# Another plan for a planned attention and MLP kernel: projections in row pieces, the first query masked by ScalarE, an exponential of zeros behind each Gelu

## The chip, the cores and the metric

The kernel runs on one core of a Trainium2 chip. A core has a matrix engine (TensorE, PE), a vector engine (VectorE, DVE), a scalar engine for activation functions (ScalarE, ACT), GpSimd (POOL), and a queue engine (SyncE, SP) that starts most transfers. The metric is the device time in microseconds from start to end of the program.

## The reference

Input x has 2048 rows of 512. One branch is an attention block with 32 heads of 16, the other a mixer MLP, and a gate mixes the two:

```
q, k, v = split(x @ wqkv)                  # 32 heads, 16 wide
a = softmax(q k^T / 4) v  @ wo             # 2048 x 2048 scores in each head
h = gelu(layernorm(x) @ w1);  hs = shift(h) @ w2;  x1 = x + hs
b = x1 + gelu(layernorm(x1) @ w3) @ w4     # 1792 wide inside
g = sigmoid(sum(x * gate_w));  out = g a + (1 - g) b
```

The scores are the bulk: 32 heads x 2048 x 2048 exponentials. The kernel cuts them into 2048 tiles of 128 keys x 512 queries.

## The kernel before

**Tiles.** A round is a chunk of 512 queries, a group of eight heads and one half of it (p); there are 32 rounds of 64 tiles. A score tile (`qk_op`, L1363; matmul on L1366) contracts over 32 rows, of which a mask leaves the 16 of one head: `qbuf` holds each query twice, once multiplied by `mE` and once by `mO`. Four score tiles can run at once on the four row tiles of TensorE (row mode). PV products and projections run as four 32-column pieces (column mode, L1590 and L999), four matmuls side by side making one step.

**Exponentials.** A tile goes one of two ways. ScalarE (`issue_act`, L1461) takes two neighbouring PSUM banks, 1024 columns, in one exponential, sometimes three or one. VectorE (`issue_dve`, L1492) writes the approximate bits of an exponential as a 16-bit integer, and three more copies shifted by multiples of 32 are made of each pair (`close_pair`), by VectorE (L1535) or GpSimd (L1537); the four PV products of these copies together approximate the exponential. So a VectorE tile costs four PV products and a ScalarE tile one.

**The rest.** Projections of q, k, v, the MLP (w1, w2, w3, w4) and the output are "gens": lists of column-mode steps into one PSUM bank, evacuated mostly by VectorE. A step over 128 rows can also be given as four 32-row pieces in row mode (`by_rows`, L1007), to row tiles that a group of scores leaves free (`Gen.row_piece`, L166); before, only the longest w4 gens can be. The first Gelu (L1233) covers all 2048 rows, the second (L1270) comes in two pairs of chunks, so ScalarE leaves its exponentials three times, and each time loads the Gelu table and then the exponential's again.

**What sets the order.** Nothing is scheduled by hand at the level of instructions. At build time a small event-driven model (`Sim`) plays the engines with fixed durations, and `pe_pick` decides at each free moment of TensorE what comes next: scores for ScalarE, scores for VectorE, PV products or a gen's steps, and fillers on zeros (L1923) where nothing is ready. The instructions are emitted in the model's order, and the hardware then runs each engine's queue in that order with semaphores. The decisions hang on knobs (`K`): a base set, and a table `STEPS` which changes some of them after every eight score tiles. For example GP3 decides how often a pair's last shifted copies stay on VectorE, DVE_STOP how many tiles of a round VectorE leaves alone at its end, ROWM how many steps a gen must have in hand before it gives one as row pieces (99 means never), SL0 and SL1 how far PE may run beyond the end of an exponential. The table was found by a search; it has 215 entries with 721 settings.

**The start.** `x_transposes` makes x^T of the first chunk, `q_proj` the first queries (16 matmuls), `k_first` the first keys in two halves of 256. The mask of the first query is split: VectorE takes columns 0 to 255 (L1086), ScalarE 256 to 511 (L1089), then ScalarE copies both key halves (L1056), and the first scores follow.

Of the kernel before, what the change touches and what calls it, by code (L numbers as in the profile page):

```python
# [452 lines left out]
def kernel(  # L453
# [87 lines left out]
        12: dict(AT_SH=0),
        13: dict(AGE=12000, ROWM=3),
        14: dict(P1_PRIO=0.312, S_PRIO=0.214, SL0=60, IDLE_NS=374, B_LOW=1, PRESS=11, MAXU=7, DUE_SH=0, HOLE=2, E_PRIO=2,
            AFIRST=2, AGE=20000, ROWM=99, ACC2=1, JOIN=0),
        16: dict(GP3=0.633, URG=2, ACC2=0),
        17: dict(GP3=0.967, DVE_STOP=6, URG=5, B_LOW=2, ACC2=1),
        18: dict(AHEAD2=16, MAXG=2),
        19: dict(SL1=130),
        20: dict(SL1=0),
        21: dict(P1_PRIO=0.279, GP2=1, GP3=0.9, DUE_SH=32),  # L550
        23: dict(GP2=0.5, ACC2=0),
        25: dict(GP3=0.633, AT_SH=69),
        26: dict(GP2=1, GP3=0.9, AT_SH=0, ACC2=1),
        27: dict(SL0=0, DUE_SH=-9),
        28: dict(DVE_STOP=13, JOIN=1),
        29: dict(DVE_STOP=6, JOIN=0),
        30: dict(ACC2=0),
        31: dict(ROT=0),
        32: dict(DVE_STOP=13, ROT=2, ACC2=1, JOIN=1),
        33: dict(P1_PRIO=0.136, AHEAD2=9),  # L560
        34: dict(P1_PRIO=0.279, AHEAD2=16),
        35: dict(ROT=3),
        36: dict(LIMA=4),
        37: dict(PV_IDLE=0.5, PRESS=18),
        41: dict(S_PRIO=0.38),
        44: dict(S_PRIO=0.178, SL1=-75, AHEAD2=24, AGE=12000),
        45: dict(ROT=1),
        46: dict(B_LOW=8),
        47: dict(GP3=0.8, DVE_STOP=4, EARLY=64, SL1=130, MAXU=2, AT_SH=118),
        48: dict(GP3=0.9, DVE_STOP=13, EARLY=99, SL1=-75, B_LOW=2, MAXU=7, ROT=3, AT_SH=0),  # L570
        50: dict(DVE_ALONE=500),
        51: dict(IDLE_NS=864, ROT=2),
        52: dict(GP3=0.967, DVE_STOP=4, DVE_STOP_L=12, URG=8, URG_L=18, DVE_ALONE=-158, IDLE_NS=700, B_LOW=3, DVE_WAIT=4,
            PV_FULL=0.916, PV_IDLE=0.117, PRESS=26, MAXU=3, ROT=0, DUE_SH=-14, AT_SH=118, HOLE=7, MAXG=1, E_PRIO=0.4,
            AFIRST=0, AGE=20000, ACC2=0, LIMA=3, JOIN=0),
        53: dict(HOLE=0),
        54: dict(DVE_ALONE=-81, MAXU=5, ROT=1),
        55: dict(URG=2, DVE_ALONE=138),
        56: dict(P1_PRIO=0.312),
        57: dict(S_PRIO=0.625, ROT=2),  # L580
        58: dict(E_PRIO=2),
        59: dict(GP2=0.655),
        60: dict(GP3=1, E_PRIO=0.4),
        61: dict(DVE_STOP_L=7, LIMD=4),
        62: dict(DVE_ALONE=2),
        63: dict(SL1=0),
        64: dict(DVE_STOP=13),
        65: dict(DVE_STOP=6, ROT=3, JOIN=1),
        66: dict(DVE_STOP=4, ROT=2, JOIN=0),
        67: dict(DVE_WAIT=3, HOLE=7),  # L590
        68: dict(GP2=1),
        69: dict(AHEAD2=13),
        70: dict(DVE_STOP_L=16, AHEAD2=24, ROT=1),
        71: dict(SL1=-75, ROT=3),
        72: dict(GP2=0.655, DVE_STOP_L=7, SL1=0, ROT=2),
        73: dict(GP2=1, AHEAD2=13),
        74: dict(P1_PRIO=0.136, S_PRIO=0.178, GP3=0.967, DVE_STOP=8, DVE_STOP_L=12, URG=5, DVE_ALONE=-158, SL1=-75,
            IDLE_NS=537, B_LOW=8, DVE_WAIT=4, AHEAD2=24, PV_IDLE=0.731, MAXU=3, ROT=3, DUE_SH=32, LIMD=3, E_PRIO=0.1,
            ROWM=7, LIMA=4),
        75: dict(S_PRIO=0.625),  # L600
        76: dict(S_PRIO=0.178),
        77: dict(LIMD=4, LIMA=2),
        79: dict(P1_PRIO=0.414, AFIRST=2, ROWM=5),
        80: dict(SL0=-75),
        82: dict(AGE=12000),
        84: dict(ROT=1),
        85: dict(HOLE=3),
        86: dict(URG=3, AFIRST=0),
        87: dict(B_LOW=0),
        88: dict(B_LOW=8),  # L610
        89: dict(B_LOW=0),
        90: dict(URG=5, B_LOW=8, AFIRST=2),
        91: dict(GP2=0.5),
        92: dict(GP2=0.8, ROT=0),
        93: dict(GP2=1, ROT=1),
        94: dict(DVE_STOP=4, DVE_WAIT=2),
        95: dict(DVE_STOP=8, DVE_STOP_L=7, DVE_WAIT=4, ROT=0),
        96: dict(GP3=0.9, DVE_ALONE=362, PRESS=18),
        97: dict(GP2=0.315, ROT=3),
        98: dict(GP2=1, ROT=0),  # L620
        99: dict(P1_PRIO=0.743, DVE_STOP_L=16, AT_SH=96, AFIRST=1),
        100: dict(P1_PRIO=0.414, GP3=0.8, DVE_STOP_L=7, ROT=1, AT_SH=118, AFIRST=2),
        101: dict(URG=11, ROWM=99),
        102: dict(P1_PRIO=0.312, GP2=0, GP3=0.967, DVE_STOP_L=12, URG=8, DVE_ALONE=500, SL1=-150, IDLE_NS=700, B_LOW=3,
            AHEAD=3, PV_FULL=0.813, PV_IDLE=0.5, PRESS=8, ROT=0, DUE_SH=-9, HOLE=0, CAP2=5, LIMD=3, E_PRIO=0.4, AGE=6000,
            ROWM=5, LIMA=3),
        105: dict(DVE_STOP=6),
        106: dict(P1_PRIO=0.414, AHEAD=5, LIMD=2),
        107: dict(LIMD=4),
        108: dict(P1_PRIO=0.312, GP3=1, URG=5, IDLE_NS=864, AHEAD=3, PV_IDLE=0.731, ROT=2, LIMD=3, AFIRST=1, LIMA=4,  # L630
            JOIN=1),
        109: dict(SL0=0, ACC2=1),
        110: dict(URG=8),
        112: dict(SL1=0, MAXG=2),
        113: dict(DVE_STOP=4),
        114: dict(S_PRIO=0.214, B_LOW=5, JOIN=0),
        116: dict(S_PRIO=0.178, IDLE_NS=537, B_LOW=3, JOIN=1),
        117: dict(PV_IDLE=0.5),
        118: dict(DVE_WAIT=2, ROT=3, DUE_SH=0),
        119: dict(P1_PRIO=0.279, GP2=0.315, GP3=0.967, URG=3, URG_L=12, DVE_ALONE=362, EARLY=64, SL0=-75, IDLE_NS=864,  # L640
            B_LOW=8, BRES=4, DVE_WAIT=3, AHEAD=9, PV_FULL=0.86, PV_IDLE=0.117, PRESS=18, MAXU=4, ROT=1, DUE_SH=-6,
            HOLE=3, MAXG=1, E_PRIO=2, AFIRST=0, AGE=20000, ROWM=7, ACC2=0, LIMA=3, JOIN=0),
        120: dict(GP3=0.8, DVE_ALONE=2),
        121: dict(SL1=-75, ROT=2),
        122: dict(GP2=0.15, GP3=0.967, URG=2, DVE_ALONE=138, SL1=0, BRES=0, DVE_WAIT=2, PV_FULL=0.947, ROT=1),
        123: dict(DVE_STOP=6, ROT=2, CAP3=6),
        124: dict(DVE_STOP=4, ROT=1, CAP3=0),
        125: dict(SL0=0, MAXU=3),
        126: dict(PRESS=11),
        127: dict(SL1=-75),  # L650
        129: dict(DVE_STOP=8, IDLE_NS=374, E_PRIO=0.25),
        130: dict(DVE_STOP=4, IDLE_NS=864, E_PRIO=2),
        131: dict(GP2=0.655, GP3=1, SL1=0, B_LOW=2, PV_FULL=0.97, PRESS=18, MAXU=4, E_PRIO=0.4),
        132: dict(DVE_STOP=8, CAP3=6),
        134: dict(ROT=3),
        136: dict(ROT=0),
        137: dict(CAP3=0),
        138: dict(SL0=-75),
        140: dict(P1_PRIO=0.312, ROT=3, DUE_SH=32),
        142: dict(P1_PRIO=0.279, ROT=0, DUE_SH=-6),  # L660
        144: dict(GP3=0.9, MAXU=3),
        145: dict(CAP2=6),
        146: dict(URG=11),
        147: dict(S_PRIO=0.38),
        148: dict(GP3=0.8),
        149: dict(GP3=0.9),
        150: dict(GP3=0.8),
        151: dict(GP2=0.8),
        152: dict(DVE_STOP=4),
        153: dict(GP3=0.9, PV_IDLE=0.5),  # L670
        155: dict(GP2=0),
        156: dict(GP2=0.8),
        157: dict(GP2=0),
        158: dict(GP2=0.8, GP3=0.8),
        160: dict(GP2=0.5),
        161: dict(GP2=0.8),
        164: dict(P1_PRIO=0.414, DVE_STOP=8, AHEAD2=16),
        165: dict(AHEAD2=13),
        166: dict(GP3=0.9),
        167: dict(P1_PRIO=0.136),  # L680
        168: dict(DVE_ALONE=-81),
        169: dict(DUE_SH=0),
        170: dict(SL0=0, IDLE_NS=459, AT_SH=69),
# [308 lines left out]
    def gen(name, at, deps, mms, N=512, due=None):  # L992
# [22 lines left out]
        if name == "w4" and len(mms) > 5:  # L1015
            g.by_rows = by_rows
# [1003 lines left out]
```

## Time and profile before

| | |
|---|---|
| median of 3 runs | 747.18 us (747.05 to 747.32) |
| the profiled execution | 746.63 us, its span 744.8 us |
| mean granted TensorE clock | 0.999 |
| TensorE, ScalarE, VectorE, GpSimd busy | 98%, 98%, 92%, 63% of the span |
| first exponential | 9.03 us |

Busy time on a page is time in which at least one instruction of the engine was under way, so where instructions overlap, the mean length of one times their number is more than the busy time. A group's row gives line, engine, operation, tiles and count, then the busy time in us and the mean length of one in ns, then the idle time before them and what ended it. A row of the timeline gives start and length in us of one instruction or of a merged run of equal ones, and in brackets the idle time before it.

### The profile page before, as it was taken

The page shows a single profiled execution, that of the slowest core. Times are in us where ns is not written, and L with a number is a line of the kernel's source. Part 1 is how long each engine was busy: PE and PEld are TensorE (multiplying, and loading weights), DVE is VectorE, ACT ScalarE, POOL GpSimd, SP SyncE. Part 2 cuts the span into 40 slices and gives each one's busy share as a digit, 9 for nine tenths or more (in the row PEclk, how much of TensorE's full clock was granted, in tenths as well). Part 3 has the DMA queues.
Part 4 walks back from the last instruction along what each step waited for, and adds up shares of the span by engine and source line. Part 5 has one row for each costly group of instructions (what it writes and reads, how often), then busy time and mean ns, then how long its engine had stood idle before and what let it go on. Part 6 is the DMA issues. An engine that isn't in the chain of part 4 may idle for free.

```text
span 744.8 us, 23763 instructions
## 1 busy us (share of the span) xinstructions
PE 732.9 (98%) x9539; PEld 215.9 (29%) x9539; DVE 682.8 (92%) x1417; ACT 730.2 (98%) x768; POOL 466.5 (63%) x464
## 2 busy tenths in 40 slices
PE   8999999999999999999999999999999999999997
PEld 5333322223322222223222222222222342222222
DVE  5999999999999999999998888999989879999996
ACT  7999999999999999999999999999999999999995
POOL 2456667778556676654566755477677785556562
PEclk9999999999999999999999999999999999999999
DMA  8512231231321220034000110011100000110001
GB/s 185 161 39 45 66 75 41 59 67 46 84 63 52 62 70 22 20 87 102 10 24 9 38 43 21 14 35 41 28 21 18 21 12 25 29 27 21 20 9 45
DMA packets 67094, 34.60 MB, mean 46 GB/s; under 512 B 46748, under 2 KB 62380, under 8 KB 66984
## 3 DMA queue, kind: packets, MB, share of 16 engines
q1 hardware_dynamic: 66040, 32.56, 17.5%
q8 instruction: 74, 1.21, 0.7%
q10 hardware_dynamic: 944, 0.52, 0.2%
q14 instruction: 36, 0.29, 0.1%
HBM read 17.40 MB, written 6.81 MB: 33 GB/s over the span
## 4 chain that ended last, share of the span: by engine, by line
PE 78%; ACT 12%; DVE 3%; issue 3%; POOL 2%; DMA 1%; SPq 0%; DVEq 0%; POOLq 0%; ACTq 0%
PE banks L1590 28%; PE banks L1366 27%; PE banks L999 22%; ACT prob L1461 11%; POOL prob L1537 1%; DVE prob L1535 1%; DVE prob L1492 1%; PE banks L978 0%; POOL oT L1629 0%; DMA pk<-den 0%; DMA bcs<-rr 0%; PE banks L1923 0%; SPq L1633 0%; PE banks L1030 0%; ACT L1461 0%
## 5 line engine op out<-in xcount | busy, mean ns | idle before, releaser
L1461 ACT ACTIVATE prob<-banks 128x1024 bf16<-128x1024 f32 x747 | 686.1, 1144 | 0.9 <-PE banks L1590 0.3
L1537 POOL TENSOR_SCALAR prob<-prob 128x1024 uint16<-128x1024 uint16 x402 | 413.5, 1046 | 240.5 <-DVE prob L1535 102.6
L1492 DVE TENSOR_SCALAR prob<-banks 128x512 uint16<-128x512 f32 x552 | 365.6, 684 | 31.1 <-PE banks L1366 24.9
L1590 PE MATMUL banks<-prob,V 128*17 128x512 bf16 (+1 forms) x3710 | 315.8, 381 | 0.6 <-POOL prob L1537 0.5
L1366 PE MATMUL banks<-q,kT 32*128 32x512 bf16 x2048 | 279.1, 384 | 4.8 <-ACT prob L1461 2.0
L1535 DVE TENSOR_SCALAR prob<-prob 128x1024 uint16<-128x1024 uint16 x429 | 166.9, 434 | 7.9 <-PE banks L1590 3.5
L1366 PEld LDWEIGHTS <-kT 32*128 32x128 bf16 x2048 | 70.6, 90 | 306.4 <-ACT prob L1461 279.1
L1590 PEld LDWEIGHTS <-V 128*17 128x17 bf16 (+1 forms) x3710 | 70.8, 88 | 118.2 <-issue 97.8
L999 PE MATMUL banks<-xnT,w 128*32 128x512 bf16 x1152 | 88.8, 383 | 0.1
L999 PE MATMUL banks<-w,hT 128*32 128x512 bf16 x688 | 59.5, 383 | 0.0
L999 PEld LDWEIGHTS <-w 128*32 128x32 bf16 x1936 | 41.0, 95 | 48.9 <-issue 28.6
L1629 POOL TENSOR_TENSOR oT<-accsb,bcs 128x512 bf16<-128x512 f32 x31 | 40.0, 1291 | 19.5 <-DVE prob L1535 9.1
L999 PE MATMUL banks<-w,w 128*32 128x256 bf16 (+1 forms) x784 | 38.8, 308 | 0.2
L999 PE MATMUL banks<-w,hB 128*32 128x512 bf16 x448 | 37.4, 382 | 0.3 <-DVE prob L1492 0.3
L1010 PE MATMUL banks<-wo,oD 32*128 32x512 bf16 x64 | 23.8, 384 | 0.0
L1611 DVE COPY accsb<-banks 128x512 f32<-128x512 f32 x31 | 21.2, 683 | 0.8 <-POOL oT L1629 0.2
L1174 DVE BATCH_NORM_STATS2 st<-x_sb 128x6 f32<-128x512 bf16 x32 | 21.3, 681 | 0.0
L999 PEld LDWEIGHTS <-hT 128*32 128x32 bf16 x688 | 14.8, 95 | 19.8 <-issue 13.1
L1263 DVE CAST hT<-banks 128x512 bf16<-128x512 f32 x28 | 19.0, 680 | 1.5 <-PE banks L999 1.5
L1263 DVE CAST hB<-banks 128x512 bf16<-128x512 f32 x28 | 19.1, 684 | 1.4 <-PE banks L999 1.3
L999 PE MATMUL banks<-w,wq 128*32 128x512 bf16 x256 | 19.6, 383 | 0.0
L999 PE MATMUL banks<-wo,oD 128*32 128x512 bf16 x176 | 19.5, 383 | 0.0
(95 smaller groups left out, 261.1 us busy)
## 6 DMA issues: line engine op xcount, KB each, us to landing
bcs<-rr SPq DMA_DIRECT2D x124, 64.0 KB
xn_dram<-xn SPq DMA_DIRECT2D x32, 128.0 KB
w<-in_B_w_dram SPq DMA_DIRECT2D x5, 512.0 KB
oD<-oT SPq DMA_DIRECT2D x124, 16.0 KB
w<-in_B_w_dram SPq DMA_DIRECT2D x4, 448.0 KB
out_dram<-ot SPq DMA_DIRECT2D x14, 128.0 KB
x_sb<-in_A_x_dram SPq DMA_DIRECT2D x3, 512.0 KB
w<-in_A_wqkv_dram SPq DMA_DIRECT2D x2, 256.0 KB
```

Of the source, the lines that this page charges most:

```text
L999: units.append([Op("col", j, lambda j=j, lf=lf, rf=rf, n0=n0, n1=n1, st=st, sp=sp: nc.tensor.matmul(get()[32 * j:32 * j + 32, n0:n1], lhsT ...
L1010: o = Op("row", i, lambda: nc.tensor.matmul(get(), lhsT=lf(0, P)[rows], rhs=rf()[rows], start=False, stop=True, tile_position=(32 * i, 0), ...
L1174: a = dve(600, deps, lambda: nc.vector.bn_stats(out=sb.slot[:], in_=x_sb[:, t, :]), prio=6, at=at, acq=[sb])
L1263: pre.append(evac(g, PSUM_NS, lambda ps, m=m: nc.vector.tensor_copy(out=h2()[:, m, :], in_=ps[:])))
L1366: o = Op("row", i, lambda: nc.tensor.matmul(dst(), lhsT=kT[G][32 * i:32 * i + 32, kt * P:(kt + 1) * P], rhs=qbuf[G, c].slot[32 * i:32 * i ...
L1461: job = act(hold, ops, lambda: nc.scalar.activation(out=prob[:, pb.cut(), :].bitcast(BF16), in_=unit()[:, rb.cut(), :], func=ACT.Exp, scal ...
L1492: return nc.vector.tensor_scalar(out=prob[:, b0.cut() if w == 2 else b0.bufs[h0].slot, :], in0=unit()[:, rb.cut() if w == 2 else rb.bufs[0 ...
L1535: return nc.vector.tensor_scalar(out=cut(k), in0=cut(0), scalar1=float(SHIFT * k), scalar2=None, op0=ALU.add)
L1537: return nc.gpsimd.tensor_scalar(out=cut(k), in0=cut(0 if both else 2), scalar1=1.0, scalar2=float(SHIFT * (k if both else 1)), op0=ALU.mu ...
L1590: return nc.tensor.matmul(one(accs[r])[32 * i:32 * i + n, :], lhsT=lhs(n), rhs=rhs(), start=st and not edge, stop=True, tile_position=(0, ...
L1611: e = dve(PSUM_NS, round_ops[r], lambda: nc.vector.tensor_copy(out=ab.slot[:], in_=one(accs[r])), acq=[ab], prio=0, frees=[accs[r], Call(a ...
L1629: n = gp(1250, d3, lambda: nc.gpsimd.tensor_tensor(out=ob.slot[:], in0=ab.slot[:], in1=bb.slot[:], op=ALU.mult), acq=[ob], frees=[ab, bb], ...
```

## The change

- The table STEPS is another one, from a short search: 184 entries with 413 settings. With it the order of nearly all the work and the split of tiles between the engines differ.
- `by_rows` is set for all gens whose name begins with w, k or q, that have more than three steps and are not of the start, instead of the long w4 gens alone.
- The mask of the first query is one ScalarE instruction over 512 columns; the first half of the first keys is copied by VectorE instead of ScalarE.
- Behind the first Gelu and behind the last Gelu of each pair, ScalarE runs an exponential of a column of zeros into a tile that is not needed any more. The model's durations for the Gelus are changed with it.

```diff
@@ STEPS (cut)
-        0: dict(GP2=0.8, DVE_STOP=13, DVE_ALONE=-158, SL0=130, B_LOW=2, PRESS=43, AGE=20000),
-        1: dict(PV_FULL=0.97, E_PRIO=0.4, JOIN=1),
...
+        81: dict(DVE_STOP=13, ROT=3, ROWM=1, ACC2=1),
+        82: dict(DVE_STOP=6, SL1=0, ROT=2, AT_SH=0, ROWM=99, ACC2=0),
...
+        124: dict(ROWM=1),
...
+        204: dict(ROT=3, AT_SH=96, ROWM=0),
...
@@ gen
-        if name == "w4" and len(mms) > 5:
+        if name[0] in "wkq" and len(mms) > 3 and at >= 0:
             g.by_rows = by_rows
@@ k_first
-            j = act(275, g.units[-1], lambda g=g, h=h: nc.scalar.copy(out=kT[0][:, 256 * h:256 * h + 256],
-                                                                      in_=one(g.buf)[:, 0:256]), prio=0, frees=[g.buf])
+            j = (act if h else dve)(275 if h else 345, g.units[-1], lambda g=g, h=h: (
+                nc.scalar.copy if h else nc.vector.tensor_copy)(out=kT[0][:, 256 * h:256 * h + 256],
+                                                                in_=one(g.buf)[:, 0:256]), prio=0, frees=[g.buf])
@@ q_proj
-            e1 = [dve(345, g.units[-1] + [j_m3], lambda: nc.vector.tensor_scalar(
-                out=qb.slot[:, 0, 0:256], in0=one(g.buf)[:, 0:256], scalar1=mE[:], scalar2=None, op0=ALU.mult), prio=0,
-                acq=[qb])]
-            e1.append(act(330, g.units[-1] + [j_m3], lambda: nc.scalar.activation(
-                out=qb.slot[:, 0, 256:512], in_=one(g.buf)[:, 256:512], func=ACT.Copy, scale=mE[:]), prio=0))
-            e1[1].need = qb
+            e1 = [act(535, g.units[-1] + [j_m3], lambda: nc.scalar.activation(
+                out=qb.slot[:, 0, :], in_=one(g.buf), func=ACT.Copy, scale=mE[:]), prio=-1, acq=[qb])]
@@ new, before mlp1
+    def gelu(ap, back):
+        g = nc.scalar.activation(out=ap, in_=ap, func=ACT.Gelu_apprx_tanh)
+        if back:
+            nc.scalar.activation(out=mb[:].bitcast(F32), in_=zero[:, 0:1], func=ACT.Exp)
+        return g
@@ mlp1
-        ge = act(93 + 1700 * KT + 3450, pre, lambda: nc.scalar.activation(
-            out=hT[:, :, 2:2 + S], in_=hT[:, :, 2:2 + S], func=ACT.Gelu_apprx_tanh), prio=0)
+        ge = act(93 + 1700 * KT + 2850, pre, lambda: gelu(hT[:, :, 2:2 + S], True), prio=0)
@@ mlp2
-            ge = act(93 + 427 * FT + (0 if n else 2750), pre, lambda h2=h2: nc.scalar.activation(
-                out=h2(), in_=h2(), func=ACT.Gelu_apprx_tanh), prio=-1)
+            back = n == len(cs) - 1
+            ge = act(93 + 427 * FT + (1310 if n == 0 else 0) + (1490 if back else 0), pre,
+                     lambda h2=h2, back=back: gelu(h2(), back), prio=-1)
```

More of the change, by code (lines that the diff above doesn't have):

```diff
@@ L541 @@
[L541 to L550, printed above, removed]
@@ L590 @@
[L590 to L599, printed above, removed]
@@ L600 @@
[L600 to L615, printed above, removed]
@@ new lines @@
+        1: dict(HOLE=3),
+        2: dict(AT_SH=118),
+        3: dict(AGE=12000),
+        4: dict(GP2=1, DVE_WAIT=1),
+        5: dict(GP2=0.5),
+        6: dict(AHEAD2=24),
+        7: dict(GP2=1, AHEAD2=13),
+        8: dict(AFIRST=1),
+        9: dict(ROT=3, DUE_SH=32, ACC2=1),
+        12: dict(DVE_STOP=8, URG=11),
+        13: dict(DVE_STOP=6, URG=5),
+        14: dict(LIMA=2),
+        18: dict(GP3=0.9),
+        20: dict(DVE_WAIT=4),
+        21: dict(SL1=-75, HOLE=2),
+        22: dict(SL1=60, HOLE=3),
@@ new lines @@
+        23: dict(SL1=-75, HOLE=2),
+        24: dict(GP2=0.5),
+        25: dict(ROT=1),
+        26: dict(MAXU=3),
+        27: dict(HOLE=3),
+        29: dict(HOLE=2),
+        30: dict(AHEAD=5),
+        32: dict(ROT=0),
+        33: dict(AHEAD=24, MAXG=2),
+        34: dict(AHEAD=5, MAXG=1, AFIRST=2),
+        35: dict(ROT=1),
+        37: dict(ACC2=0),
+        40: dict(URG=8),
+        43: dict(E_PRIO=0.1),
+        44: dict(E_PRIO=2),
+        45: dict(ROT=2),
+        46: dict(DVE_ALONE=-81, MAXU=7),
@@ new lines @@
+        60: dict(P1_PRIO=0.312),
+        61: dict(GP2=1),
+        63: dict(DVE_WAIT=1),
+        64: dict(PRESS=15, ROT=0),
+        65: dict(DVE_WAIT=4, PRESS=18, ROT=2),
+        66: dict(P1_PRIO=0.55),
+        67: dict(P1_PRIO=0.312),
+        69: dict(HOLE=7),
+        70: dict(DVE_STOP_L=12, IDLE_NS=459, B_LOW=8, JOIN=1),
+        72: dict(DVE_STOP_L=14, IDLE_NS=374, B_LOW=3, JOIN=0),
+        73: dict(ROT=1),
+        74: dict(DVE_STOP_L=12, IDLE_NS=459, B_LOW=8, ROT=2, JOIN=1),
+        76: dict(PV_FULL=0.813, MAXG=2),
@@ new lines @@
+        97: dict(GP3=0.9),
+        99: dict(E_PRIO=0.1),
+        101: dict(GP3=0.967),
+        102: dict(GP3=0.9, E_PRIO=2),
+        103: dict(AFIRST=0),
+        104: dict(GP2=0),
+        105: dict(DVE_ALONE=500),
+        106: dict(DUE_SH=-6),
+        108: dict(HOLE=7),
+        109: dict(MAXU=2),
+        111: dict(ROT=1),
+        112: dict(URG=3, SL0=-75, PV_IDLE=0.5),
+        113: dict(MAXU=9, LIMD=4, LIMA=4),
+        115: dict(GP3=1, MAXG=2),
+        116: dict(EARLY=64, PRESS=26, LIMA=2),
@@ new lines @@
+        126: dict(DVE_STOP_L=7, CAP2=5),
+        127: dict(DVE_STOP_L=14, CAP2=6),
+        128: dict(SL1=0),
+        129: dict(URG_L=18, SL0=0),
+        131: dict(DVE_WAIT=4, E_PRIO=0.25),
+        132: dict(AT_SH=118),
+        133: dict(ROT=1, AGE=3000),
+        134: dict(PV_FULL=0.86),
+        137: dict(PV_FULL=0.916, ROT=2, AGE=9000),
+        138: dict(PV_FULL=0.86, ROT=1, AGE=3000),
+        141: dict(PV_FULL=0.916, ROT=2, AGE=9000),
+        144: dict(GP2=0.8),
+        146: dict(BRES=2, AT_SH=0),
@@ new lines @@
+        148: dict(PV_FULL=0.813, GATE=3),
+        149: dict(GP2=0.655, GP3=1, BRES=0, PV_FULL=0.916, AT_SH=118, GATE=2),
+        150: dict(GP2=0.8, GP3=0.967),
+        151: dict(GP2=0, URG_L=12, SL0=45, SL1=60, DVE_WAIT=3, AT_SH=0, E_PRIO=2, ROWM=99),
+        152: dict(DVE_STOP=4, URG_L=18, PV_IDLE=0.117, MAXU=4),
+        153: dict(ROWM=3),
+        154: dict(URG=2),
+        155: dict(GP2=1, URG=5),
+        156: dict(AT_SH=118),
+        157: dict(AT_SH=0),
+        158: dict(LIMD=4),
+        160: dict(LIMD=3),
@@ new lines @@
+        161: dict(IDLE_NS=459, AHEAD=3),
+        162: dict(URG=3),
+        163: dict(URG=5),
+        164: dict(DVE_STOP=6, SL0=60),
+        165: dict(AFIRST=2),
+        166: dict(E_PRIO=0.4),
+        167: dict(GP2=0.655),
+        169: dict(GP2=0, URG_L=12, SL0=45, IDLE_NS=537, AHEAD=9, PV_IDLE=0.731, MAXU=9, E_PRIO=2, AFIRST=0, ROWM=99),
+        170: dict(GP2=1, URG_L=18, SL0=60, IDLE_NS=459, AHEAD=3, PV_IDLE=0.117, MAXU=4, AFIRST=2, ROWM=3),
+        171: dict(E_PRIO=0.4),
+        172: dict(S_PRIO=0.3, IDLE_NS=864),
@@ new lines @@
+        173: dict(P1_PRIO=0.279, AHEAD2=24),
+        176: dict(DVE_STOP_L=12, URG_L=12, ROT=0, AT_SH=96),
+        178: dict(URG=11, AT_SH=69, AFIRST=0),
+        179: dict(MAXG=2),
+        180: dict(URG=5, AT_SH=96, MAXG=1, AFIRST=2),
+        182: dict(AT_SH=34),
+        183: dict(S_PRIO=0.178),
+        184: dict(IDLE_NS=374, AT_SH=96),
+        185: dict(AHEAD=7),
+        186: dict(HOLE=0),
+        187: dict(URG=11, LIMD=4),
+        189: dict(DVE_ALONE=500),
+        190: dict(P1_PRIO=0.55, URG_L=18, SL0=0),
@@ new lines @@
+        192: dict(P1_PRIO=0.279, GP2=0.315),
+        193: dict(PRESS=8),
+        194: dict(AT_SH=118, AFIRST=0),
+        195: dict(SL0=-150, DUE_SH=32),
+        197: dict(P1_PRIO=0.414, S_PRIO=0.38, DVE_STOP_L=14, URG=5, URG_L=12, DVE_ALONE=2, SL0=45, IDLE_NS=537, AHEAD=9,
+            AHEAD2=13, PV_IDLE=0.731, PRESS=18, MAXU=9, ROT=2, DUE_SH=-14, AT_SH=0, HOLE=3, LIMD=3, E_PRIO=2, ROWM=99),
+        199: dict(GP2=0, HOLE=7),
+        200: dict(E_PRIO=0.4),
+        201: dict(GP2=1, E_PRIO=2),
@@ new lines @@
+        202: dict(AT_SH=34),
+        203: dict(AHEAD2=16),
+        204: dict(ROT=3, AT_SH=96, ROWM=0),
+        205: dict(DVE_STOP_L=7, ROT=0),
+        208: dict(GP2=0.315),
+        209: dict(GP3=0.8, AHEAD=12),
+        210: dict(GP2=0, GP3=0.967, DVE_STOP_L=14, AHEAD=9, AHEAD2=13, ROT=2, AT_SH=0, ROWM=99),
+        211: dict(ROWM=3),
+        213: dict(ROT=0, LIMA=4),
+        214: dict(PV_FULL=0.86),
+        217: dict(AHEAD=12, MAXU=2),
+        219: dict(S_PRIO=0.3, CAP2=5),
+        221: dict(ROT=3),
@@ new lines @@
+        225: dict(PRESS=8),
+        226: dict(S_PRIO=0.38, BRES=4, ROT=1),
+        227: dict(SL0=130),
+        228: dict(S_PRIO=0.3, SL0=45, BRES=0, MAXU=4, ROT=3),
+        229: dict(MAXU=2),
+        231: dict(S_PRIO=0.38, SL0=130, BRES=4, ROT=1),
+        232: dict(S_PRIO=0.3, GP2=0.315, SL0=45, SL1=-75, BRES=0, ROT=3),
+        233: dict(GP2=0, SL1=60, MAXU=4),
+        234: dict(MAXU=2),
+        235: dict(ROT=0),
+        237: dict(ROT=2),
+        240: dict(URG=11, URG_L=18),
+        241: dict(URG=5, URG_L=12),
```

238 lines of the change are left out of this document (39 added, 199 removed).

## The prediction

> **What bounds the kernel now.** I read the page's busy shares first, then the groups of instructions, then single stretches of the timeline, because three engines look full at once.
>
> ```profile
> span 744.8 us, 23763 instructions
> PE 732.9 (98%) x9539; PEld 215.9 (29%) x9539; DVE 682.8 (92%) x1417; ACT 730.2 (98%) x768; POOL 466.5 (63%) x464
> PE 78%; ACT 12%; DVE 3%; issue 3%; POOL 2%; DMA 1%; SPq 0%; DVEq 0%; POOLq 0%; ACTq 0%
> L1461 ACT ACTIVATE prob<-banks 128x1024 bf16<-128x1024 f32 x747 | 686.1, 1144 | 0.9 <-PE banks L1590 0.3
> ```
>
> The chain of waits gives 78% to TensorE, but matmuls are pipelined and follow each other through ScalarE's releases, so the chain alone cannot say which of the two is full. ScalarE's line can. The groups by form, the timeline and the list of waits:
>
> ```profile
> L1461 ACT ACTIVATE prob<-banks 128x1024 bf16<-128x1024 f32 x745 | 684.4, 1144 | 0.9 <-PE banks L1590 0.3 <-PE banks L1366 0.2
> L1461 ACT ACTIVATE prob<-banks 128x1536 bf16<-128x1536 f32 x1 | 1.5, 1458 | 0.0
> L1461 ACT ACTIVATE prob<-banks 128x512 bf16<-128x512 f32 x1 | 0.8, 778 | 0.0
> ...
> 360.65 1.02 ACT L1461 ACTIVATE prob<-banks 128x1024 bf16<-128x1024 f32 x1
> 362.47 13.87 ACT L1461 ACTIVATE prob<-banks 128x1024 bf16<-128x1024 f32 x15
> 460.05 13.89 ACT L1461 ACTIVATE prob<-banks 128x1024 bf16<-128x1024 f32 x15
> ...
> PEld L1366 <- ACT prob L1461: 279.1, 636, 1.4
> ```
>
> One exponential alone lasts 1.02 us; fifteen in a row last 13.87 us, so each further one adds (13.87 - 1.02) / 14 = 0.918 us. Over the whole run, 684.4 us of occupied time over 745 exponentials is 0.9187 us each. The mean of the run is the pace of an undisturbed stretch: apart from the 0.9 us of idle time shown, ScalarE is never late. Of the score groups on TensorE (702 in the built instruction stream of the kernel before), 636 wait for an exponential to free PSUM banks. So TensorE is paced by ScalarE, not the other way round, and the time is the number of exponentials times 0.9187 us, plus the Gelus with their table loads, the start and the end.
>
> **The change, part by part.** Counts of the changed kernel are from its built instruction stream; durations are from the profile.
>
> Other plan, exponentials. A tile of scores is exponentiated on ScalarE, or approximated on VectorE. ScalarE had 1494 of 2048 tiles (745 wide instructions, one of three tiles, one of one); now it has 1504, in 752 wide ones. VectorE has 544 instead of 554. ScalarE: 752 x 0.9187 = 690.9 us against the 686.1 us that all 747 took: +4.8 us. All of it is on the path, since that row has no idle time to fill. Bounds: +4.6 at 0.918 with nothing else, +4.8 at the mean; I take +4.8.
>
> Other plan, the other engines:
>
> ```profile
> L1492 DVE TENSOR_SCALAR prob<-banks 128x512 uint16<-128x512 f32 x550 | 363.3, 682 | 31.0 <-PE banks L1366 24.9 <-ACT prob L1461 1.7
> L1492 DVE TENSOR_SCALAR prob<-banks 128x1024 uint16<-128x1024 f32 x2 | 2.4, 1219 | 0.0
> L1535 DVE TENSOR_SCALAR prob<-prob 128x1024 uint16<-128x1024 uint16 x429 | 166.9, 434 | 7.9 <-PE banks L1590 3.5 <-ACT prob L1461 1.6 <-POOL prob L1537 0.6
> L1537 POOL TENSOR_SCALAR prob<-prob 128x1024 uint16<-128x1024 uint16 x402 | 413.5, 1046 | 240.5 <-DVE prob L1535 102.6 <-PE banks L1590 38.4 <-DVE prob L1492 24.6
> ...
> 164.84 0.61 PE L1590 MATMUL banks<-prob,V 128*17 128x512 bf16 x8
> 165.44 0.39 PE L1366 MATMUL banks<-q,kT 32*128 32x512 bf16 x2
> 165.75 0.61 PE L1590 MATMUL banks<-prob,V 128*17 128x512 bf16 x8
> 166.35 0.39 PE L1366 MATMUL banks<-q,kT 32*128 32x512 bf16 x3
> ```
>
> VectorE: single tiles 550 to 536 (14 x 363.3/550 = -9.2 us), double tiles 2 to 4 (+2.4), shifted copies 429 to 453 (24 x 166.9/429 = +9.3): +2.5 us on an engine with 62 us idle, so nothing directly. GpSimd: shifted copies 402 to 363, 39 x 413.5/402 = -40 us; it is 37% idle, so no gain. TensorE: groups in row mode 702 to 716, steps in them 708 to 730, column-mode steps 1825 to 1818. A group takes 0.31 us until column work starts behind it (165.44 to 165.75), so 14 more are +4.3 us; eight second steps and the seven fewer column steps nearly cancel, at about the same price each. The way back into row mode costs something too: eight matmuls on four tiles are two steps, and take 0.60 us to the next group. TensorE gets +4 to +7 us. It is hidden while ScalarE is the later one, and ScalarE itself gets +4.8 us in which to hide it; the cover is thin, about a tie. If it fails in places, exponentials come late. Price of that: at the low end -0.5 us (745 x 0.0007, all lateness in today's mean gone), at the high end +6 us (what TensorE gets at most, less part of the cover). I take +1.2 us, nearer the low end, because 636 of 702 groups wait for ScalarE now. The filler matmuls on zeros go from 72 to 128, but all stand beside Gelus, where TensorE has nothing else: nothing.
>
> Projections in 32-row pieces. The built streams have 84 such pieces instead of 80: 12 new ones for an MLP projection, 8 fewer for the output projection. A piece needs a step left over and a knob (ROWM) at 0 or 1 for four-step projections, and the table has that for a few stretches only. One column step of some 1818: nothing.
>
> First query masked by ScalarE, half of the first key copy on VectorE. The timeline of the start, and a 512-wide ScalarE instruction of that kind from the end of the kernel:
>
> ```profile
> 6.04 1.14 PE L999 MATMUL banks<-w,wq 128*32 128x512 bf16 x16
> 6.99 1.06 PE L999 MATMUL banks<-w,w 128*32 128x256 bf16 x32
> 7.29 0.48 DVE L1086 TENSOR_SCALAR q<-banks,mE 128x256 bf16<-128x256 f32 x1 [0.72 <-PE banks L999]
> 7.81 0.47 ACT L1089 ACTIVATE q<-banks,mE 128x256 bf16<-128x256 f32 x1 [1.30 <-DVE q L1086]
> 8.18 0.64 ACT L1056 CAST kT<-banks 128x256 bf16<-128x256 f32 x2
> 8.32 0.75 DVE L1092 TENSOR_SCALAR q<-banks,mO 128x512 bf16<-128x512 f32 x1 [0.54 <-ACT q L1089]
> 8.60 0.40 PE L1366 MATMUL banks<-q,kT 32*128 32x512 bf16 x4 [0.55 <-ACT kT L1056]
> 9.03 2.86 ACT L1461 ACTIVATE prob<-banks 128x1024 bf16<-128x1024 f32 x3 [0.21 <-PE banks L1366]
> ```
>
> Today the two halves of the mask run one after the other, then the key copies. New: ScalarE masks all 512 columns from 7.29 on, in about 0.7 us, to 7.98; VectorE copies the first key half meanwhile, from about 7.6 (half of the 32 matmuls) to 8.1. The first scores start at about 8.15 instead of 8.60, and the first exponential 0.45 us earlier. ScalarE runs without a pause from there, so it counts: -0.5 us, between that and 0, should the next scores be late instead (they need the second key half, which ScalarE now copies alone behind the mask).
>
> The Trainium skill ("ScalarE: Activation LUTs", Rules for kernel authors) says the opposite of this edit: multiplications belong on VectorE, which it calls up to about three times faster. The rows disagree here: 256 columns out of PSUM take 0.48 us on VectorE and 0.47 us on ScalarE. By the page the mask would take up to three times VectorE's 0.75 us and this term would be about +1.1 us instead of -0.5 us.
>
> Exponential of zeros behind Gelu. Today the table load that brings the exponential back stands behind the wait of the next real exponential; now a tiny exponential carries it directly behind the Gelu.
>
> ```profile
> 352.34 6.16 ACT L1270 ACTIVATE hT<-hT 128x7168 bf16<-128x7168 bf16 x1
> 358.55 0.39 PE L1366 MATMUL banks<-q,kT 32*128 32x512 bf16 x2
> 359.35 1.28 ACT L1461 ACT_TABLE_LOAD   x1 [0.85 <-PE banks L1590]
> ...
> L1461 ACT ACT_TABLE_LOAD x3 | 3.8, 1283 | 0.9 <-PE banks L1590 0.8
> L974 ACT ACTIVATE zc<-zero 128x1 f32<-128x1 bf16 x1 | 0.2, 203 | 0.0
> ```
>
> The three loads waited 0.9 us together, 0.85 of it in one place; that is all there is to win. Three tiny exponentials cost 3 x 0.2 = 0.6 us. Net -0.3 us, between -0.9 (they overlap their neighbours) and +0.6 (the waits go on behind them).
>
> The end. From 735.0 to 744.8 us no exponential sets the time but a fixed chain of VectorE and TensorE steps, with the same instructions in both kernels.
>
> ```profile
> 733.68 0.38 PE L1366 MATMUL banks<-q,kT 32*128 32x512 bf16 x1
> 733.99 2.12 PE L1590 MATMUL banks<-prob,V 128*17 128x512 bf16 x22
> 735.00:744.80 9.80, 5.13 (x66) 2.18 (x58) 4.55 (x10) 2.21 (x4) 0.00 (x0) 0.90 0.16 54
> 730.17 0.68 DVE L1299 TENSOR_TENSOR w<-w,banks 128x512 f32<-128x512 f32 x1
> ```
>
> Fewer PV matmuls are left behind the last scores (13 instead of about 30: up to -1.0 us), but one sum of 0.68 us on VectorE has moved from well before the end to just before the last transposes. I take 0, between -1.0 and +0.7.
>
> Sum: 4.8 + 1.2 - 0.5 - 0.3 + 0 = +5.2 us. The profiled execution took 746.63 us (span 744.8), so 751.8 us; the median of the runs lies 0.55 us above that execution, which gives 752.4 us.
>
> **Rivals.** The change in a median that can be told from none is about 0.2%, 1.5 us here.
>
> Late exponentials become the rule. A plan that asks more of all three full engines lets ScalarE wait. For it: TensorE's +4 to +7 us against +4.8 us of cover, and VectorE at 92%. Against: the 636 waits for ScalarE. Price: the whole +7 us of TensorE exposed on top of the sum's 4.0 us without lateness, or more: 756 to 765 us.
>
> The savings cancel it. Lateness -0.5, start -0.5, Gelu -0.9, end -1.0 leave 4.8 - 2.9 = +1.9 us at best, 749.1 us; a measurement within 1.5 us of before needs a little more than every lower bound at once.
>
> Faster: the 0.918 us are not the engine's own pace but contain waiting that a plan can take out. It decides at 686.1/752 = 0.9124 us an exponential: below that the ten added tiles are free. The Trainium skill ("Perfetto Trace Analysis", Optimizing Scalar/DVE Operations) gives ScalarE about 51 ns of access time on PSUM, and "ScalarE: Activation LUTs" (What ACT_TABLE_LOAD costs) 1 element per cycle at 1.2 GHz; the estimate from these is 0.904 us for 1024 columns, and by it the time would be some 11 us shorter than the sum, 741 us. Worked out from rows alone: at 0.9124 us, with the start and Gelu savings taken, the time is 746.4 us, and each 0.001 us less takes off another 0.75 us. Against it: two stretches of fifteen, 100 us apart, show the same 0.918 and 0.919 us, and so does the whole run. A wait would not be that even.
>
> **How the numbers follow.** Forecast, 749 to 756 us: 0.72. Late exponentials, 756 to 765 us: 0.16. No change, 745.7 to 748.7 us: 0.07. Faster: 0.05. So faster 0.05, same 0.07, slower 0.88. The range starts at 748.7 us, just under the sum of the lower bounds, and goes to 758.5 us, into the late rival; it leaves out faster, no change and the far half of the late rival, some 0.2.
>
> **What would show it.** In the profile after: ScalarE's exponential row x752 with about 691 us (plan); if it stays under 687 us, the pace was not a floor. Its idle time under 2 us and a mean of 0.917 to 0.921 us confirm the lateness term; 0.925 or more is the late rival. The first exponential near 8.6 us (start). A load right at the end of each Gelu without idle time, and a tiny exponential of 0.2 us (Gelu). About 9.8 us from the last exponentials to the end (tail). The prediction fails if TensorE's added groups are what ScalarE waits for, or if the pace falls with GpSimd's 40 us of writes gone.

## The result, and the profile after

The changed kernel takes 751.02 us (median of 4, 750.47 to 751.34) against 747.12 us for the kernel before; the ratio is 1.0042, with a 95% interval of 1.0026 to 1.0057. It is slower by 0.3 to 0.6%; the two medians alone stand at 1.0052, inside that interval. The forecast was 752.4 us in a range of 748.7 to 758.5, so way and size came out, the size 1.4 us too high. The profiled execution took 750.47 us, its span is 748.7 us, 3.9 us more than before.

The page of the changed kernel: busy shares, and the chain of waits by engine.

```profile
span 748.7 us, 23793 instructions
PE 737.7 (99%) x9565; PEld 213.0 (28%) x9565; DVE 684.6 (91%) x1429; ACT 735.2 (98%) x775; POOL 426.2 (57%) x425
PE 56%; ACT 9%; DVE 2%; issue 2%; POOL 1%; ACTq 0%; DVEq 0%; POOLq 0%
```

ScalarE's and VectorE's groups by form (busy us, mean ns of one, idle time before), GpSimd's largest, and the list of waits:

```profile
L1414 ACT ACTIVATE prob<-banks 128x1024 bf16<-128x1024 f32 x752 | 690.6, 1148 | 1.9 <-PE banks L1319 1.5
L1163 ACT ACT_TABLE_LOAD x3 | 3.8, 1283 | 0.0
L1163 ACT ACTIVATE mb<-zero 128x1 f32<-128x1 bf16 x3 | 0.6, 203 | 0.0
L1445 DVE TENSOR_SCALAR prob<-banks 128x512 uint16<-128x512 f32 x536 | 354.7, 683 | 36.7 <-PE banks L1319 32.1 <-ACT prob L1414 0.6
L1488 DVE TENSOR_SCALAR prob<-prob 128x1024 uint16<-128x1024 uint16 x453 | 178.5, 438 | 5.1 <-PE banks L1543 1.9 <-ACT prob L1414 0.4 <-POOL prob L1490 0.4
L1490 POOL TENSOR_SCALAR prob<-prob 128x1024 uint16<-128x1024 uint16 x363 | 373.6, 1044 | 275.0 <-DVE prob L1488 152.7 <-DVE prob L1445 32.7 <-PE banks L1319 27.4
PEld L1319 <- ACT prob L1414: 283.2, 647, 1.0
```

The exponentials take 690.6 us instead of 686.1: +4.5 us, somewhat more than the slowdown. Per instruction it is 690.6 / 752 = 0.9184 us, the pace of before. GpSimd is 40 us less busy, and the pace of the exponentials is no faster for it. The chain's 56% for TensorE would point to the wrong engine again.

The start, one Gelu and the last exponentials, in the timeline of the changed kernel:

```profile
5.73 1.10 PE L949 MATMUL banks<-w,wq 128*32 128x512 bf16 x16
6.88 0.69 ACT L1037 ACTIVATE q<-banks,mE 128x512 bf16<-128x512 f32 x1 [0.71 <-PE banks L949]
7.32 0.42 DVE L1006 CAST kT<-banks 128x256 bf16<-128x256 f32 x1 [1.13 <-PE banks L949]
7.80 0.40 PE L1319 MATMUL banks<-q,kT 32*128 32x512 bf16 x4
8.23 1.94 ACT L1414 ACTIVATE prob<-banks 128x1024 bf16<-128x1024 f32 x2
...
361.42 6.17 ACT L1161 ACTIVATE hT<-hT 128x7168 bf16<-128x7168 bf16 x1
367.59 1.28 ACT L1163 ACT_TABLE_LOAD   x1
368.88 0.20 ACT L1163 ACTIVATE mb<-zero 128x1 f32<-128x1 bf16 x1
368.99 1.92 ACT L1414 ACTIVATE prob<-banks 128x1024 bf16<-128x1024 f32 x2
...
736.45 3.94 ACT L1414 ACTIVATE prob<-banks 128x1024 bf16<-128x1024 f32 x4
```

The first exponential comes at 8.23 instead of 9.03 us: 0.4 us by the edits (from the first mask on it is 8.23 - 6.88 = 1.35 us instead of 9.03 - 7.29 = 1.74), and 0.4 us because the first query's product was ready earlier in this execution, ahead of any edit (the mask starts at 6.88 instead of 7.29). That second half is chance as far as the profiles show: the instructions ahead are the same, and in the other profiles with the new start the mask starts between 6.76 and 7.79 us, in those with the old one between 7.43 and 7.74. The table load follows its Gelu at once; the tiny exponential's 0.20 us overlap, so the next one starts 0.11 us after it (368.88 to 368.99). The last exponential ends at 740.4 us, 8.3 us before the end, where it was 8.9 us before (735.9 of 744.8).

The rows account for most of the 3.9 us: +4.5 (exponentials), +1.0 (idle ahead of them, 1.9 instead of 0.9), -0.9 and +0.3 (the waits of the three loads, three tiny exponentials), -0.8 (start) and -0.6 (end), together +3.5 us. The other 0.4 us lie in the rounding and overlap of rows, as the sums over ScalarE's whole stretch show. From the start of the first exponential to the end of the last, 732.16 us instead of 726.91, ScalarE is busy for 730.26 us instead of 725.28 and idle for 1.90 instead of 1.63. So +5.0 us of ScalarE's work, +0.3 of its idle time, -0.8 at the start and -0.6 at the end make the 3.9 us.

### The profile page after: what moved, and what is told of

Same layout as the page of the kernel before. It is cut to its first block, busy times and chain, and to the rows that moved or that the text cites. A ratio compares the mean times of both kernels' runs of the same rounds, so it can differ in the third digit from the quotient of the medians.

```text
span 748.7 us, 23793 instructions
## 1 busy us (share of the span) xinstructions
PE 737.7 (99%) x9565; PEld 213.0 (28%) x9565; DVE 684.6 (91%) x1429; ACT 735.2 (98%) x775; POOL 426.2 (57%) x425
## 4 chain that ended last, share of the span: by engine, by line
PE 56%; ACT 9%; DVE 2%; issue 2%; POOL 1%; ACTq 0%; DVEq 0%; POOLq 0%
PE banks L1543 20%; PE banks L1319 20%; PE banks L949 15%; ACT prob L1414 6%; ACT hB L1161 2%; POOL prob L1490 1%; DVE prob L1488 1%; DVE prob L1445 0%; ACT L1161 0%; DVE hT L1215 0%; DVE accsb L1920 0%; DVE accsb L1923 0%; ACT xn L1939 0%; PE banks L1936 0%; PE banks L1897 0%
## 5 line engine op out<-in xcount | busy, mean ns | idle before, releaser
L1414 ACT ACTIVATE prob<-banks 128x1024 bf16<-128x1024 f32 x752 | 690.6, 1148 | 1.9 <-PE banks L1319 1.5
L1490 POOL TENSOR_SCALAR prob<-prob 128x1024 uint16<-128x1024 uint16 x363 | 373.6, 1044 | 275.0 <-DVE prob L1488 152.7
L1445 DVE TENSOR_SCALAR prob<-banks 128x512 uint16<-128x512 f32 (+1 forms) x540 | 359.5, 687 | 37.1 <-PE banks L1319 32.5
L1543 PE MATMUL banks<-prob,V 128*17 128x512 bf16 (+1 forms) x3680 | 317.4, 381 | 0.2 <-DVE prob L1488 0.2
L1319 PE MATMUL banks<-q,kT 32*128 32x512 bf16 x2048 | 285.9, 384 | 3.7 <-ACT prob L1414 1.3
L1488 DVE TENSOR_SCALAR prob<-prob 128x1024 uint16<-128x1024 uint16 x453 | 178.5, 438 | 5.1 <-PE banks L1543 1.9
L949 PE MATMUL banks<-xnT,w 128*32 128x512 bf16 x1140 | 95.1, 383 | 0.0
L949 PE MATMUL banks<-w,hT 128*32 128x512 bf16 x688 | 63.5, 383 | 0.0
L1582 POOL TENSOR_TENSOR oT<-accsb,bcs 128x512 bf16<-128x512 f32 x31 | 39.5, 1273 | 30.3 <-DVE prob L1488 11.8
L949 PE MATMUL banks<-wo,oD 128*32 128x512 bf16 x184 | 21.5, 383 | 0.2 <-issue 0.2
L960 PE MATMUL banks<-wo,oD 32*128 32x512 bf16 x56 | 20.8, 384 | 0.0
L1161 ACT ACTIVATE hT<-hT 128x7168 bf16<-128x7168 bf16 (+1 forms) x3 | 19.4, 6453 | 0.0
```

What stands on the lines that cost most here:

```text
L949: units.append([Op("col", j, lambda j=j, lf=lf, rf=rf, n0=n0, n1=n1, st=st, sp=sp: nc.tensor.matmul(get()[32 * j:32 * j + 32, n0:n1], lhsT ...
L960: o = Op("row", i, lambda: nc.tensor.matmul(get(), lhsT=lf(0, P)[rows], rhs=rf()[rows], start=False, stop=True, tile_position=(32 * i, 0), ...
L1161: g = nc.scalar.activation(out=ap, in_=ap, func=ACT.Gelu_apprx_tanh)
L1319: o = Op("row", i, lambda: nc.tensor.matmul(dst(), lhsT=kT[G][32 * i:32 * i + 32, kt * P:(kt + 1) * P], rhs=qbuf[G, c].slot[32 * i:32 * i ...
L1414: job = act(hold, ops, lambda: nc.scalar.activation(out=prob[:, pb.cut(), :].bitcast(BF16), in_=unit()[:, rb.cut(), :], func=ACT.Exp, scal ...
L1445: return nc.vector.tensor_scalar(out=prob[:, b0.cut() if w == 2 else b0.bufs[h0].slot, :], in0=unit()[:, rb.cut() if w == 2 else rb.bufs[0 ...
```

## The experiments

Theory: ScalarE's exponentials run at the engine's own pace without a break, so a microsecond more on ScalarE is one more of the time; the new table puts ten more tiles there. Rivals: the pace contains waiting or contention; TensorE sets it; the code edits cost, not the table. The kernel before was measured again beside each series; its medians lie between 747.15 and 747.42 us.

**Is 0.917 us ScalarE's own pace?** A kernel with nothing but the exponentials, alternating over four pairs of banks:

```diff
+for n in range(400):
+    k = 2 * (n % 4)
+    nc.scalar.activation(out=prob[:, k:k + 2, :], in_=bk[:, k:k + 2, :], func=ACT.Exp, scale=0.25)
```

> Leaves the whole computation out: ScalarE alone runs 400 exponentials of 1024 columns from PSUM to SBUF, nothing beside it. Theory (the pace in the kernel is ScalarE's own): 0.917 us from one to the next, so the row of 400 is occupied for about 367 us. Rival (0.904 us is its own, the rest is waiting or contention): about 362 us.

Its group, and the first twenty in its timeline:

```profile
L39 ACT ACTIVATE prob<-banks 128x1024 bf16<-128x1024 f32 x400 | 366.8, 2938 | 0.2 <-PE banks L36 0.2
2.25 18.44 ACT L39 ACTIVATE prob<-banks 128x1024 bf16<-128x1024 f32 x20 [0.24 <-PE banks L36]
```

366.8 / 400 = 0.917 us, with no other engine at work beside them (one execution). The pace is ScalarE's own, and the rival that ended on the fast side is gone. The mean length of one, 2938 ns, shows what that column is worth: in the first stretch the starts come 0.904 us apart and the ends 0.917, so each instruction is recorded longer than the one before it, at an unchanged pace.

**More work on ScalarE alone, more on TensorE alone.** Both on the kernel before, whose order stays as it was.

```diff
# b_plus_act, in issue_act: ahead of every 50th exponential
+                for _ in range(4):
+                    nc.scalar.activation(out=mb[:].bitcast(F32), in_=zero[:, 0:1], func=ACT.Exp)
# b_plus_pe, in take_pv: behind every 60th PV product, a product with zeros
+                m = nc.tensor.matmul(one(accs[r])[32 * i:32 * i + DH + 1, 0:384], lhsT=zero[:, 0:DH + 1], rhs=zero[:], start=False, ...
```

> The kernel before with the same plan; ahead of every 50th exponential four tiny exponentials of zeros (60 in all, in 15 places). One takes 0.11 us of ScalarE's time in the changed kernel: about 6.6 us more for ScalarE, about as much as seven exponentials, nothing for the others. Theory (every microsecond on ScalarE is one of the time): 753.3 to 754.5 us. Rival (ScalarE follows another engine): 749 us or less.

> The kernel before with the same plan; behind every 60th PV product one more matmul of 384 columns on zeros on the same tile (59 in all). A step with it lasts about 0.16 us longer: up to 9.4 us more for TensorE, nothing for the others. Theory (TensorE is covered, with 0.05 to 0.1 us of room in a cycle of one exponential): most of it hidden, 747 to 750 us. Rival (TensorE sets the pace as well): 753 us or more.

Four tiny exponentials in a row do not overlap and take more than expected; that the common output column is the reason was not tested. The timeline of the first place, and the group:

```profile
26.89 0.92 ACT L1467 ACTIVATE mb<-zero 128x1 f32<-128x1 bf16 x4
27.71 1.92 ACT L1468 ACTIVATE prob<-banks 128x1024 bf16<-128x1024 f32 x2
...
L1467 ACT ACTIVATE mb<-zero 128x1 f32<-128x1 bf16 x60 | 13.5, 225 | 1.4
```

From the ends of the exponentials around them, each of the 15 places costs ScalarE 0.78 us, 11.7 us in all. The time rose from 747.28 to 759.07 us (ratio 1.0149, 1.0123 to 1.0174): 11.8 us, one for one. The products with zeros, up to 9.4 us more for TensorE by the estimate above (the row of PV products grew from 315.8 to 321.4 us), gave 748.91 us (1.0021, 1.0011 to 1.0032): 1.6 us, the rest hidden. The size expected for the first was wrong, the rule held.

**Less work on ScalarE, less on TensorE, both.** On the changed kernel, order unchanged. Half of the columns of 38 tiles, or the last 64 queries of each chunk in all PV products but the first of a sum, are not computed.

```diff
# a_act_cut, in issue_act: every 40th exponential (19)
+                return nc.scalar.activation(out=prob[:, pb.cut(), 0:256].bitcast(BF16),
+                                            in_=unit()[:, rb.cut(), 0:256], func=ACT.Exp, scale=0.25)
# a_pe_cut, in take_pv
+            cols = 512 if st or edge else 448
+            return nc.tensor.matmul(one(accs[r])[32 * i:32 * i + n, 0:cols], lhsT=lhs(n), rhs=rhs()[:, 0:cols], ...
```

> The changed kernel with the same order everywhere; every 40th exponential (19 in all) covers only the first 256 columns of each of its two tiles, so half of those 38 tiles is not computed. This takes 19 x 512 columns = 8.1 us at one column per 0.833 ns from ScalarE and nothing from any other engine. Theory (ScalarE's count sets the time): 751.0 - 8 = 743 us, at least 6 us of it seen. Rival (TensorE or VectorE set it, ScalarE only follows): 750 to 751 us.

> The changed kernel with the same order everywhere; all PV products but the first of each sum cover 448 of 512 columns, so the last 64 queries of each chunk are left out. About 890 steps of TensorE become 64 columns shorter: some 24 us less for TensorE, nothing for the others. Theory (TensorE is covered): gain of at most the 1.9 us that exponentials sat idle plus the few late ones and the last steps, 747 to 751 us. Rival (TensorE sets the pace): 741 us or less.

> The changed kernel with the same order and both cuts: 19 exponentials over half their columns (8.1 us off ScalarE) and PV products over 448 of 512 columns (about 24 us off TensorE); half of 38 tiles and the last 64 queries of each chunk are left out. Alone the first cut gave 3.5 us, the second 0.5 us. Theory (ScalarE is first, TensorE stands only a few us behind and took the rest of the first cut): more than the 4.0 us of the two together, 743 to 745.5 us. Rival (VectorE or the transfers took the rest): 747 us, as with the first cut alone.

Less TensorE work: 750.50 us, 1.0046 (1.0029 to 1.0062) of the kernel before, which cannot be told from the changed kernel's 1.0042. The row of PV products had fallen from 317.4 to 291.8 us. TensorE does not set the time. Less ScalarE work: 747.55 us, 3.5 us gained of 8.1, under the 6 us that I had set. Both: 746.48 us, about 1 us less than the first cut alone; so TensorE's throughput holds back at most about 1 of the 4.6 us that are missing, and that expectation missed too. The time lies nearer to its rival's 747 us. The timeline around one cut (688.04) in a_act_cut shows what did:

```profile
686.23 2.08 ACT L1422 ACTIVATE prob<-banks 128x1024 bf16<-128x1024 f32 x2
688.04 0.76 ACT L1420 ACTIVATE prob<-banks 128x512 bf16<-128x512 f32 x1
688.37 0.38 PE L1320 MATMUL banks<-q,kT 32*128 32x512 bf16 x1
688.87 2.85 ACT L1422 ACTIVATE prob<-banks 128x1024 bf16<-128x1024 f32 x3
```

The full exponential ahead of the cut one ends at 688.31 us and frees its banks; the next scores start at 688.37, and the exponential that reads them at 688.87. This round trip of 0.56 us from bank to bank hides behind an exponential of 0.92 us, but not behind one of 0.49 us. Over all 19 cuts the next exponential ended 1.11 us after the cut one on average instead of 0.917: 0.20 us lost of each 0.43 us saved, 3.7 of the 4.6 us. Of these 0.20 us about 0.11 are the restart (an exponential after a pause takes 1.02 us) and 0.09 are waiting. The round trip was 0.49 to 0.71 us, 0.58 on average; in five of the cuts TensorE began the scores 0.2 us or more after the banks were free, in the others within 0.13 us. With TensorE's work cut too the average was 0.56. ScalarE is first, with a latency close behind it and in a few places TensorE's order; TensorE's throughput is not what stands second. VectorE, 91% busy, was not varied by a run of its own. Of the 36.7 us that it is idle ahead of its single tiles it waits 32.1 us for scores from TensorE, which speaks against it as the limit but does not settle it.

**The three exponentials of zeros.** Taken out of the changed kernel, and added to the kernel before, the order unchanged in both.

```diff
# a_nodummy
-        if back:
+        if False:
             nc.scalar.activation(out=mb[:].bitcast(F32), in_=zero[:, 0:1], func=ACT.Exp)
# b_dummy: the function gelu as in the change, called with the model's durations of before
```

> The changed kernel without the three exponentials of zeros, the same order otherwise. Theory (worth -0.3 us net in the prediction): 751.0 + 0.3, so 750.8 to 751.8 us; the loads go back behind the wait of the next exponential, and idle time shows ahead of them only where the scores come late. Rival (the load ahead of the wait is worth more, because the scores come late at all three places): 752.5 us or more.

> The kernel before with the same plan, only the three exponentials of zeros behind the Gelus added. The loads waited 0.87 us there and each small exponential takes 0.11 us of ScalarE's time in the changed kernel: 747.15 - 0.87 + 0.33 = 746.6 us. Rival (the waits only move behind the small exponential): 747.5 us.

Without them the changed kernel takes 752.35 us, 1.3 us more, above the expected 0.3 and its range; the load behind the first Gelu waits 0.94 us, and the three wait 1.7 us together:

```profile
184.67 1.28 ACT L1414 ACT_TABLE_LOAD   x1 [0.94 <-PE banks L1543]
...
L1414 ACT ACT_TABLE_LOAD x3 | 3.8, 1283 | 1.7 <-PE banks L1543 1.7
```

1.7 - 3 x 0.11 = 1.4 us. With them the kernel before takes 746.84 us (0.9988, 0.9979 to 0.9997): 0.5 us less, as expected. What such an exponential is worth is the wait of the load in that plan.

**The edits without the table.** The kernel before with the start's edits and the exponentials of zeros; the plan comes out the same.

> The kernel before with the same plan; the first query masked by ScalarE, the first key half copied by VectorE, and the three exponentials of zeros. Theory (both edits are worth what the traces say, -0.5 and -0.5 us, and the table alone costs): 746.1 us, faster than both kernels. Rival (an earlier start is lost to late scores soon after): 746.6 to 747.2 us.

746.13 us against 747.33 us of the same chip: 0.9984 (0.9975 to 0.9993), the fastest of all. Against the exponentials of zeros alone it is 0.7 us, but the two intervals overlap. The first exponential starts at 8.50 us, 0.5 us earlier than in the profile of before:

```profile
7.15 0.69 ACT L1087 ACTIVATE q<-banks,mE 128x512 bf16<-128x512 f32 x1 [0.71 <-PE banks L999]
8.50 1.94 ACT L1462 ACTIVATE prob<-banks 128x1024 bf16<-128x1024 f32 x2
```

The rule for row pieces does nothing here: with the old table the built streams of all engines are the same with and without it. So the edits gain 1.2 us, and the new table, with the rule and the durations that it was planned with, costs about 5 us; the rival that blamed the edits is gone for the two kernels compared here.

**The table.** The tables cannot be exchanged: the model of either code comes to a stop with the other's. So both codes were planned with an empty one (`STEPS = {}`), and the changed code with its table but the old rule for row pieces.

> The code before with an empty table of knobs: 761 exponentials of 1024 columns (1522 tiles on ScalarE). Theory (time goes by ScalarE's count): 16 wide ones more at 0.917, less the two odd ones, +12.8 us: 760.0 us, plus late exponentials, so 760 to 764 us. Rival (count does not decide): no relation, under 757 or over 768 us.

> The changed code with an empty table of knobs: 759 exponentials of 1024 columns and one of 512 (1519 tiles on ScalarE), no row pieces at all. Theory (time goes by ScalarE's count, the code edits gain about 1 us): 6.9 us over the changed kernel's 751.0, 757.9 us, plus late exponentials, so 757.5 to 761 us, and 2 to 4 us under the code before with an empty table. Rival (the code edits, not the table, cost the 3.9 us): over the code before with an empty table.

> The changed kernel with the same table, row pieces allowed for the long w4 gens alone as before. The plan comes out otherwise: 757 exponentials instead of 752, 140 fillers. Theory: +4.6 us by the count, and lateness because the table was found with the new rule: 755.5 to 765 us. Rival (row pieces for other projections are of no use): 751 us or less.

776.96 us and 786.61 us: both expectations missed, by 13 us and more, and both times came out where the rival had put them. The page of either (code before, then changed) says why, in the last column:

```profile
L1223 ACT ACTIVATE prob<-banks 128x1024 bf16<-128x1024 f32 x761 | 700.5, 1133 | 17.2 <-PE banks L1128 9.6 <-PE banks L1352 6.8 <-ACT prob L1223 0.6
```

```profile
L1226 ACT ACTIVATE prob<-banks 128x1024 bf16<-128x1024 f32 x759 | 699.2, 1122 | 27.3 <-PE banks L1355 13.1 <-PE banks L1131 9.1 <-issue 4.2
```

Against the kernel before, the first has +14.4 us of exponentials and +16.3 us of idle time ahead of them, 30.7 us together, where the span grew by 775.2 - 744.8 = 30.4 us. The second has +13.1 and +26.4, 39.5 us, and its span grew by 39.7 us. The sum of the two columns gives the time of both plans; the count alone does so only where late ones are few. With the old rule for row pieces the changed code takes 760.83 us with 757 exponentials, within the expectation: 4.6 us by the count and some 5 us beyond it.

```profile
L1414 ACT ACTIVATE prob<-banks 128x1024 bf16<-128x1024 f32 x757 | 695.5, 1143 | 6.0 <-PE banks L1543 2.5
```

Against the changed kernel that is +4.9 us of exponentials and +4.1 us of idle time; the span grew by 10.0 us. The table was searched with one rule, and another rule gives another plan; that the pieces as such are worth 9.8 us does not follow. Whether a long search would make the new code faster than the best kernel here stays open. That the edits cost without a table (10 us between the two empty ones) is a matter of idle time in two plans that no search has touched, and the run does not separate edit from chance.

## Why the prediction was right

**The bound.** It rested on the equality of two numbers, 0.918 us in a stretch and 0.9187 us over the run. The exponentials alone (0.917 us) and the tiny ones (11.8 us for 11.7) show that both it and its consequence hold. The estimate from the two pages of the Trainium skill that the prediction names ("Perfetto Trace Analysis" and "ScalarE: Activation LUTs") was 0.904 us; the measurement decides for 0.917.

**The exponentials' term.** +4.8 was forecast, +4.5 measured (690.6 against 686.1 us).

**Late exponentials.** +1.2 forecast; +1.0 us of idle time. The cover of TensorE was called thin, about a tie; it is thicker than that: up to 9.4 us more gave 1.6 us on the kernel before, and work taken from TensorE gave nothing that can be told from noise on the changed one. My price, +4 to +7 us of TensorE, was right as work (its busy time rose from 732.9 to 737.7 us) and far too high as risk.

**Gelu.** -0.3 forecast; -0.9 + 0.3 = -0.6 between the two traces, because a tiny exponential costs 0.11 and not 0.2 us. Measured by itself on the kernel before: -0.5 us. The new plan would have waited 1.7 us at these places, so in it the edit is worth 1.3 us.

**Start.** -0.5 forecast, -0.4 us by the edits; the first exponential came another 0.4 us earlier in the profiled execution, and that was luck. VectorE copied the key half in 0.42 us beside ScalarE's mask of 0.69 us; the mask on ScalarE is not slower than VectorE's 0.74 us for the other mask over the same 512 columns, so the rule of the Trainium skill ("ScalarE: Activation LUTs", Rules for kernel authors) that puts multiplications on VectorE gains nothing for this operation out of PSUM. The rule gives its factor of three for bf16, and this source is f32; the prediction took the factor over without that condition.

**End.** 0 forecast, -0.6. In the kernel before, then in the changed one:

```profile
734.26 1.68 ACT L1461 ACTIVATE prob<-banks 128x1024 bf16<-128x1024 f32 x2
737.02 0.72 DVE L1967 STREAM_TRANSPOSE accsb<-banks 128x512 f32<-128x512 f32 x1 [1.49 <-PE banks L1590]
...
740.90 0.72 DVE L1920 STREAM_TRANSPOSE accsb<-banks 128x512 f32<-128x512 f32 x1 [2.64 <-PE banks L1543]
```

The gain lies between the last exponential and the first transpose, 0.5 instead of 1.1 us; from there on both take 7.8 us. So of the two bounds the one from fewer PV products was the nearer; the sum that moved ahead of the transposes ended at 738.26 us, before they began. The prediction began this stretch at 735.0 us, where two exponentials still run (until 735.94): its sign, about 9.8 us from the last exponentials to the end, fits neither kernel (8.9 and 8.3 us).

No single step failed. In the profiled execution the total came out 1.3 us too high: the end gave 0.6 us more than its term, the Gelus 0.3 and lateness 0.2, the exponentials 0.3 less than forecast, and the 0.4 us of luck at the start went the same way; the start's edits erred the other way, and the rows leave 0.4 us over. The rivals: more late exponentials did not happen, but the empty tables show that the mechanism is there and can cost 16 to 26 us; no change would have needed all savings at once, and start, Gelu and end together came to 2.0 us.

## What to carry to other kernels

Find the engine whose mean over the run equals the pace of an undisturbed stretch; there a changed plan can be priced by counting instructions in the built stream, as long as its idle column stays where it was. Read count and idle time together: each alone misses, as the empty tables show. A tiny instruction that carries a table load ahead of a wait is worth what the load waited, no more.

## What the runs showed that was not expected

- The recorded length of an exponential grows when many follow each other: 1.02 us for one after a pause, 1144 ns on average in the kernel before, 2938 ns alone at the same pace of 0.917 us. Only ends, or the busy time of a row, give the pace.
- A table load behind a Gelu follows it at once, 361.42 + 6.17 = 367.59 us, and the next exponential comes at its end. The Trainium skill ("ScalarE: Activation LUTs", What ACT_TABLE_LOAD costs) adds some 1.4 us of draining to the load; the trace shows 1.28 us for the load and none beside it here. In the kernel before, one of the three return loads waited 0.85 us for TensorE.
- Two bank pairs give a round trip of 0.49 to 0.71 us from the end of an exponential to the start of the one that reads the same banks next, and an exponential after a pause takes 1.02 us, so a shorter exponential gains less than its columns.
- Tiny exponentials into the same column take 0.23 us each in a row, against 0.11 us for one ahead of a full one; why was not tested.
